# Where the rows of the first two groups are finished: part of a tuned spectral-filter and feed-forward kernel is moved into an earlier stage

## The chip, the cores and the metric

The kernel runs on one core of one Trainium2 chip. Its time is the device time of one execution in microseconds (us); the median of three runs of the kernel before is 159.57 us (159.57 to 159.85). The engines are TensorE (PE; its weight loads are listed as PEld), VectorE (DVE), ScalarE (ACT), GpSimd (POOL) and the sync engine (SP), whose queue issues the DMAs. Each engine carries out its own instructions in the order in which the program has them and waits on semaphores for the others.

## The reference

```
h   = x + irfft2( rfft2(layernorm(x)) * (w_r + i w_i) )       x: 1 x 2048 x 512, bf16
out = h + ( relu(layernorm(h) @ w1 + b1) ** 2 ) @ w2 + b2     w1: 512 x 1792, w2: 1792 x 512
```

The Fourier transforms are taken over rows and columns (2048 and 512) and are made of matrix products with tables of sines. h stands for the filtered rows; the second line is a feed-forward network, with a residual h and a bias b2 added to each output row.

## The kernel before, in words

The 2048 rows are 16 groups of 128 (row = 16 p + g), g = 0 to 15, with p on the partitions. The kernel has three runs, one behind the other.

The first run loads x, makes the tables, takes the statistics of the first layer norm and does the first transform steps.

The middle run (lines 508 to 772) goes over eight pairs of row frequencies, pr = 0 to 7. For each, TensorE makes p2 (lines 522 to 532) and p3 (573 to 600), ScalarE copies them out as U and AB, VectorE makes X (sums and differences), m (times the filter weights), Z and M (lines 607 to 653), TensorE makes p4 (655 to 685) and ScalarE copies it to T2 (687 to 700). Pair 7 comes last, and its p4 is made in two parts: "a" holds only what groups 0 and 1 need (copied by T2a-7), "b" the rest (T2b-7-0 and T2b-7-1). Groups 0 and 1 then get a short path of their own, so that the feed-forward part can start: pd (line 703) multiplies T2 by the inverse column table GI, EO (710) copies it out, yt (714 to 736) adds the filter result to the transposed x, sq, ss, sd and r2 (737 to 748) take the second layer norm's factor, and UT0 (750) is the normalised input of the feed-forward part, transposed. GI is scaled in place on GpSimd (line 495) after two DMA transposes have brought it.

The last run (lines 774 to 1001) works in five chunks of groups, (0,1), (2..4), (5..8), (9..12), (13..15). For chunk 0 the up products ph (line 949) read UT0; the first two of its fourteen are split by group, pf-0 and pf-1 for group 0, ph-0-0 and ph-0-1 for group 1. For each later group, p5 (814) and p6 (837) finish the filter, with od, q and R between them; hs is the row h. relu (962), squares (967), the down products po (978) and the output addition ot (988) follow; ot adds hb, which is h + b2. For chunk 0, hb is made from py (lines 875 to 892): three steps of products add x (an identity product), and two parts of the filter result in EO, and VectorE adds the bias b2b. That is done in the last run, at its beginning.

The order of the instructions on an engine is set by a planner, class Plan (line 34). Every step is a task with an estimated duration, what it reads and writes, and a priority; run() always takes the task that can start first. Where an order is written out by hand, in MID (line 760) for the middle run and DRAIN (line 995) for the beginning of the last, the planner follows it. SP and POOL have no written order: there priorities, estimated durations and the estimated time to landing ("lag") decide. The planner also puts in products of a zero tile fz (warm(), line 244; they compute nothing that is used) where it sees TensorE wait over 0.3 us.

PSUM has eight banks. In the middle run the pool psg holds two single banks (0 and 1), and psb three pairs of banks (2-3, 4-5, 6-7) for "mm" tiles. In the last run the pool ps2 has four single banks, 2 to 5, for p5, p6 and some of ph ("pp" and "ph" tiles), and pso has banks 6 and 7 for "po" tiles. Lines 774 and 778 to 779 change the pools; a tile of ps2 or pso may be written when the tile of psb that lay there has been read out (reuse_waits="tile"). Before, py is a "po" tile.

Of the kernel before, what the change touches and what calls it, by code (L numbers as in the profile page):

```python
# [9 lines left out]
ALU = mybir.AluOpType  # L10
ACT = mybir.ActivationFunctionType
# [4 lines left out]
P = 128  # L16
# [17 lines left out]
class Plan:  # L34
# [13 lines left out]
    def add(self, eng, w, fn, reads=(), writes=(), prio=0.0, alloc=None, at=0.0, shared=False, lag=0.0,  # L48
            uses=(), order=(), name=None):
        many = isinstance(eng, tuple)  # L50
        ways = dict(zip(eng, w)) if many else {eng: w}
        t = dict(many=many, eng=None, ways=ways, w=0.0, fn=fn, reads=list(reads), writes=list(writes), prio=prio, alloc=alloc, at=at,
                 shared=shared, lag=lag, end=None, order=list(order), n=len(self.tasks),
                 name=name or "-".join(map(str, writes[-1] if isinstance(writes[-1], tuple) else writes[-1:])))
        self.tasks.append(t)
        for k in t["writes"]:
            self.made.setdefault(k, []).append(t)
        for k in set(t["reads"]) | set(t["writes"]) | set(uses):
            self.use.setdefault(k, []).append(t)
# [85 lines left out]
def kernel(  # L145
# [52 lines left out]
    sq0 = persist.tile([P, 2, ND, P], BF16, name="sq0")  # L198
    rsb = persist.tile([P, 2, P], FP32, name="rsb")
    UT0 = persist.tile([P, 2, ND, P], BF16, name="UT0")  # L200
    EO = persist.tile([P, 2, 2, 256], BF16, name="EO")
    junk = persist.tile([P, D], BF16, name="junk")
    fz = persist.tile([P, 512], BF16, name="fz")
# [30 lines left out]
    psg = ps  # L234
# [7 lines left out]
    add = plan.add  # L242

    def warm(p):
        for _ in range(min(7 if psg is ps else 20, int(plan.gap * 0.6 / 0.0625)) if plan.gap > 0.3 else 0):
            mm(p[:, 0:P], lhsT=fz[:, 0:P], rhs=fz[:, 0:P], start=True, stop=True)  # L246

    def sg_tile(key):
# [44 lines left out]
    def pool(w, fn, prio, reads=(), writes=(), **k):  # L293
        add("POOL", w, fn, reads=reads, writes=writes, prio=prio, **k)
# [167 lines left out]
            order=[("EI", 3)], writes=[("EI", 3, pr)], prio=17, lag=6.0)  # L462
    for t in range(2):
        add("SP", 1.3, lambda t=t: sy.dma_start(GI[:, :, P * t:P * t + P], flat(GF[:, t]), transpose=True), reads=[("gf", t)],
            order=[("EI", 3)], writes=[("gi", t)], prio=40.5 + t / 10, lag=12.0)
    for k, (d, s) in ((0, (W1[:], B_w1.rearrange("(c p) f -> p c f", p=P))),
                      (1, (W2[:], B_w2.rearrange("(i p) d -> p i d", p=P))),
                      (3, (b2b[:], B_b2.unsqueeze(0).to_broadcast([P, D])))):
        add("SP", 0.7, lambda d=d, s=s: sy.dma_start(d, s), writes=[("FW", k)], prio=40 + k, lag=15.0,
            order=[("gi", 1)] * (k > 0) + [("EI", i) for i in range(4)] + [("Wr", 0), ("Wr", 1), ("Wn", 0), ("Wn", 1)])  # L470

    PE0 = 5
    BY_PE = tuple(range(PE0, 8))
# [7 lines left out]
    def mid_tasks():  # L481
        def b1t():
            p = sg_tile(("b1",))
            mm(p[:, 0:NF], lhsT=b1b[:], rhs=ident[0:NF, 0:NF], start=True, stop=True)
            for g in range(2):
                mm(p[0:2, P + P * g:2 * P + P * g], lhsT=nmh[:, g], rhs=ident[:], start=True, stop=True)
        act(0.19, lambda: sc.copy(nmt[:], T[("b1",)][0:2, P:3 * P].rearrange("p (g c) -> p g c", g=2)), 142.0, reads=[("b1",)],
            writes=["nmt"], name="nmt")
        add("PE", 0.2, b1t, reads=["b1b", "ident", "nmh"], order=[("p3", 3)], writes=[("b1",)], prio=141.0, alloc=("sg", ("b1",)))
        act(0.19, lambda: sc.copy(b1f[:], T[("b1",)][:, 0:NF]), 142.0, reads=[("b1",)], writes=["b1f"])  # L490
        act(1.4, lambda: sc.preload_act_table_set("natural_log_exp_and_others"), 0.0, reads=["eps"], writes=["sqrt"])

        pool(0.2, lambda: gp.memset(ones[:], 1.0), 400.0, writes=["ones"])
        for e in range(2):
            pool(0.5, lambda e=e: gp.tensor_scalar(GI[:, 1 + 2 * e], GI[:, 1 + 2 * e], hrow[:], 1.0, ALU.mult, ALU.mult), 410.0,  # L495
                 reads=["hv", ("gi", 0), ("gi", 1)], writes=["GI"], name=f"GI-{e}")
        pool(0.15, lambda: gp.tensor_copy(nmh[:, :, 0], nm1[:, 0:2]), 401.0, reads=["nm1"], writes=["nmh0"])
        pool(0.15, lambda: gp.tensor_tensor(nmh[:, :, 1], nm1[:, 0:2], nmh[:, :, 0], ALU.subtract), 402.0, reads=["nmh0"],
             writes=["nmh"])
# [218 lines left out]
        for d in range(ND):  # L718
            mm(T["yt", g][:, P * d:P * d + P], lhsT=xs[:, g, P * d:P * d + P], rhs=ident[:], start=False, stop=False)
    for g in range(2):  # L720
        add("PE", 0.22, lambda g=g: cen(g), reads=["ones", "nmt"], order=[("p3", 7)], writes=[("yt", g, 0)],
            uses=[("yt", g)], name=f"yt-{g}-0", prio=170.0, alloc=("sg", ("yt", g)))
        add("PE", 0.22, lambda g=g: res(g), reads=["ident"], order=[("yt", g, 0)], uses=[("yt", g)],
            writes=[("yt", g, 1)], name=f"yt-{g}-1", prio=170.0)

    for g in range(2):
# [23 lines left out]
        def ut0(g=g):  # L750
# [2 lines left out]
        dve(0.66, ut0, -30.0, reads=[("r2", 0, g)], uses=[("yt", g)],   # L753
            writes=[("UT", 0), "UT0b" if g else "UT0a"], name=f"UT0-{g}")

    def sq_of(src, g):
        sc.activation(junk[:], src, ACT.Square, bias=nm1[:, g:g + 1], accum_out=ss2[:, g:g + 1])  # L757

    T["UT", 0] = UT0
    MID = {  # L760
# [10 lines left out]
    }  # L771
    plan.run(MID)

# [26 lines left out]
    ONE = (1, 2, 3, 4)  # L800
    TURN = (2, *range(5, G))
    HBP = 0
    OWN = 1
    SPLIT = 2
    UPT = ("ph", "sg")

    for c, (a, b) in enumerate(CHUNKS):
# [64 lines left out]
                add(("DVE", "POOL")[HBP], (0.62, 1.3)[HBP], lambda g=g: (ve, gp)[HBP].tensor_tensor(hb[:, g, :], hs[:, g, :], b2b[:], ALU.add),  # L872
                    prio=late + 180 + g, reads=[("hs", g), ("FW", 3)], order=[("ph", c, 4)], writes=[("hb", g)])

        if c == 0:
            for g in range(2):
                def d6(g=g, k=0):
                    py = (bank(("py", g), "po", 2) if k == 0 else T["py", g])[:]
                    if k == 0:
                        mm(py, lhsT=ident[:], rhs=xs[:, g, :], start=True, stop=False)  # L880
                    elif k == 1:
                        mm(py, lhsT=KI[:, 0], rhs=EO[:, g, 0].unsqueeze(1).to_broadcast([P, 2, 256]), start=False, stop=False)
                    else:
                        mm(py[:, 0:256], lhsT=KI[:, 0], rhs=EO[:, g, 1], start=False, stop=False)
                        mm(py[:, 256:512], lhsT=KI[:, 1], rhs=EO[:, g, 1], start=False, stop=True)
                for k in range(3):
                    add("PE", 0.22, lambda g=g, k=k, d6=d6: d6(g, k), reads=[["ident"], [("EO", g), ("EI", 3)], [("EO", g)]][k],
                        order=[("yt", 1, 3)] + [("py", g, j) for j in range(k)], uses=[("py", g)],
                        writes=[("py", g, k)] + [("py", g)] * (k == 2), name=f"py-{g}-{k}", prio=-3000.0 + g,
                        alloc=None if k else ("po", ("py", g)))  # L890
                dve(0.69, lambda g=g: ve.tensor_tensor(hb[:, g, :], T["py", g][:], b2b[:], ALU.add), -10.0,
                    reads=[("py", g), ("FW", 3)], order=[("UT", 0)] * OWN, writes=[("hb", g)])
        else:
            z = late + 50
            for k, (p0, p1) in enumerate([(g, g + 1) for g in range(a, b)] if c in ONE else [(a, b)]):
                pool(0.15, lambda p0=p0, p1=p1: gp.tensor_scalar(rs2[:, p0:p1], ss2[:, p0:p1], 1.0 / D, EPS, ALU.mult, ALU.add),  # L896
# [76 lines left out]
        for i in range(n):  # L973
            g = a + i
            for h in range(2) if g == G - 1 else (None,):
# [9 lines left out]
                        writes=[("po", g, h), ("po", g, h, k)], uses=[("act", c)], prio=nxt(),  # L985
                        alloc=("po", ("po", g, h)) if k == 0 else None)

                def out_(g=g, h=h, cs=cs):
                    o = T["ot", g] if h else buf(ffn, ("ot", g), "ot", [P, D], BF16, 3)
                    ve.tensor_tensor(o[:, cs], T["po", g, h][:, cs], hb[:, g, cs], ALU.add)  # L990
                dve(0.66 if h is None else 0.42, out_, nxt(), reads=[("po", g, h), ("hb", g)], uses=[("ot", g)],
                    writes=[("ot", g, h)], alloc=None if h else ("ot", ("ot", g)))
                add("SP", 0.1, lambda g=g, cs=cs: sy.dma_start(ov[:, g, cs], T["ot", g][:, cs]), reads=[("ot", g, h)],
                    writes=[("out", g)], uses=[("ot", g)], prio=nxt())
    DRAIN = {
        "PE": "py-1-0 py-0-0 py-1-1 py-0-1 py-1-2 py-0-2 pf-0 pf-1 p5-2 ph-0-0 ph-0-1 p5-3 ph-0-5 "
             "ph-0-3 ph-0-2",
        "ACT": "od-2 rl-0-0 rl-0-1 od-3 rl-0-5",
        "DVE": "hb-1 hb-0 q-2-0 q-2-1",
    }  # L1000
    plan.run(DRAIN)
    pin(tc, nc)
# [29 lines left out]
```

## Time and profile before

| what | value |
|---|---|
| median of three runs | 159.57 us |
| the profiled execution: its time, its span | 158.99 us, 157.2 us |
| busy: TensorE, VectorE, ScalarE, GpSimd | 152.0, 116.4, 102.0, 37.7 us |
| granted TensorE clock | 1.0 |
| middle run's last VectorE step (M-7-1) ends | 43.5 us |
| first feed-forward product starts | 49.5 us |
| zero-tile products (L246) in all | 69, of which 10 behind the middle run's main part |

The span is the profiled part of the execution; 1.79 us lie around it. "L952" and the like are lines of the kernel. A busy figure is a sum over the span, so a stage has to be read for itself. The view of stretches gives the busy time of each engine between two moments; the chain of waits is followed back from the last instruction to what released each step; the timeline lists an engine's instructions with start, length, and the idle time ahead of them with what ended it.

### The profile page before, as it was taken

Reading aid. Unit: us, or ns where it says so; the run is one execution under the profiler, and the core shown is the slowest. Engines: PE = TensorE matmul, PEld = TensorE weight load, DVE = VectorE, ACT = ScalarE, POOL = GpSimd, SP = SyncE. Lnnn points to the kernel's source line nnn. Section 1 sums busy time; section 2 is a strip of 40 time slices with the busy share of each in tenths; the row PEclk is TensorE's granted clock in tenths of the full one; section 3 lists DMA queues with packets and bytes.
Section 4 is the critical chain, followed back from the end, with each engine's and each line's share of the span. In section 5 each row is a group of like instructions: output and inputs, shape, how many; then the busy total and the mean of one; then the engine's idle time right before and its main releaser. Section 6 shows DMA issues by size and latency. Waiting matters only on the chain.

```text
span 157.2 us, 2915 instructions
## 1 busy us (share of the span) xinstructions
PE 152.0 (97%) x1038; PEld 92.5 (59%) x1038; DVE 116.4 (74%) x310; ACT 102.0 (65%) x187; POOL 37.7 (24%) x84
## 2 busy tenths in 40 slices
PE   6998999999999999999999999999999999999992
PEld 4677876787788985556544544444544444555461
DVE  6999889999908987899832989981699963285221
ACT  8989689999767996599702889340688820288000
POOL 8898300005900024213400022530002340000000
PEclk9999999999999999999999999999999999999999
DMA  4957998799700001121121000324000412100011
GB/s 151 312 190 222 284 224 176 210 295 310 226 4 0 4 0 35 48 54 38 33 67 60 7 4 0 67 48 120 33 0 4 66 38 65 35 33 4 0 67 33
DMA packets 23449, 14.02 MB, mean 89 GB/s; under 512 B 12170, under 2 KB 22154, under 8 KB 23434
## 3 DMA queue, kind: packets, MB, share of 16 engines
q1 hardware_dynamic: 23434, 13.84, 33.5%
q8 instruction: 8, 0.13, 0.3%
q14 instruction: 7, 0.06, 0.1%
HBM read 8.92 MB, written 3.01 MB: 76 GB/s over the span
## 4 chain that ended last, share of the span: by engine, by line
PE 75%; DVE 14%; issue 3%; POOL 3%; DMA 2%; ACT 0%; DVEq 0%
PE po L981 31%; PE sg L952 20%; PE ph L952 11%; DVE Z L635 4%; DVE m L625 4%; DMA xs<-in_A_x_dram 2%; DVE X L611 2%; DVE st L395 2%; POOL KR L411 1%; PE pp L840 1%; DVE M L649 1%; DVE M L647 1%; POOL rs L402 1%; PE pp L847 1%; PE s_p L418 1%
## 5 line engine op out<-in xcount | busy, mean ns | idle before, releaser
L981 PE MATMUL po<-W,act 128*128 128x512 bf16 (+1 forms) x238 | 50.0, 367 | 0.0
L964 ACT ACTIVATE rl<-sg,b1f 128x512 bf16<-128x512 f32 (+2 forms) x46 | 27.4, 602 | 20.1 <-PE sg L952 19.1
L952 PEld LDWEIGHTS <-W 128*128 128x128 bf16 x288 | 26.9, 98 | 19.3
L952 PE MATMUL sg<-UT,W 128*128 128x512 bf16 (+3 forms) x188 | 37.6, 334 | 0.0
L981 PEld LDWEIGHTS <-act 128*128 128x128 bf16 x238 | 23.1, 98 | 24.3
L970 DVE TENSOR_TENSOR act<-rl 128x384 bf16<-128x384 bf16 (+2 forms) x70 | 25.2, 368 | 6.5 <-ACT rl L964 6.0
L990 DVE TENSOR_TENSOR ot<-po,hb 128x512 bf16<-128x512 f32 (+1 forms) x17 | 11.2, 660 | 22.0 <-PE po L981 21.9
L896 POOL TENSOR_SCALAR rs<-ss 128x1 f32<-128x1 f32 x14 | 5.8, 416 | 65.5 <-ACT junk L757 65.5
L952 PE MATMUL ph<-UT,W 128*128 128x384 bf16 (+3 forms) x100 | 20.5, 328 | 0.0
L964 ACT ACTIVATE rl<-ph,b1f 128x384 bf16<-128x384 f32 (+2 forms) x24 | 14.3, 596 | 8.2 <-PE ph L952 7.5
L757 ACT ACTIVATE junk<-hs,nm 128x512 bf16<-128x512 bf16 x14 | 10.0, 714 | 1.7 <-DVE hs L868 1.5
L868 DVE TENSOR_TENSOR hs<-pp,xs 128x512 bf16<-128x512 f32 x14 | 9.6, 689 | 1.8 <-PE pp L840 1.3
L495 POOL TENSOR_SCALAR GI<-GI,hrow 128x256 bf16<-128x256 bf16 x2 | 6.0, 2986 | 17.5 <-DMA GI<-GF 17.5
L506 PE MATMUL m_p<-U,EF 128*128 128x512 bf16 (+1 forms) x46 | 9.5, 337 | 0.0
L863 DVE TENSOR_TENSOR R<-q 128x127 bf16<-128x127 f32 x40 | 9.3, 285 | 0.0
L872 DVE TENSOR_TENSOR hb<-hs,b2b 128x512 f32<-128x512 bf16 x14 | 9.2, 684 | 0.0
L395 DVE BATCH_NORM_STATS2 st<-xs 128x6 f32<-128x512 bf16 x14 | 9.0, 672 | 0.1
L898 POOL TENSOR_TENSOR rs<-rs,mhalf 128x1 f32<-128x1 f32 x14 | 8.3, 596 | 1.2
L689 ACT CAST T<-m_p 128x1024 bf16<-128x1024 f32 (+1 forms) x8 | 7.5, 955 | 0.8 <-PE m_p L673 0.7
L908 ACT ACTIVATE u<-hs,nr,rs 128x512 bf16<-128x512 bf16 x5 | 4.1, 811 | 5.9 <-POOL nr L900 5.9
L246 PEld LDWEIGHTS <-fz 128*128 128x128 bf16 x69 | 5.5, 108 | 3.8 <-issue 1.6
L830 DVE TENSOR_TENSOR q<-pp,od 128x256 f32<-128x256 f32 x20 | 7.7, 417 | 0.0
(154 smaller groups left out, 230.4 us busy)
## 6 DMA issues: line engine op xcount, KB each, us to landing
W<-in_B_w_dram SPq DMA_DIRECT2D x2, 1792.0 KB, 8.5
out_dram<-ot SPq DMA_DIRECT2D x15, 128.0 KB, 1.8
xs<-in_A_x_dram SPq DMA_DIRECT2D x4, 256.0 KB, 3.6
xs<-in_A_x_dram SPq DMA_DIRECT2D x2, 512.0 KB, 6.1
W<-wx SPq DMA_DIRECT2D x2, 448.0 KB, 5.1
W<-in_A_w_r_dram SPq DMA_DIRECT2D x1, 512.0 KB, 8.6
W<-in_A_w_i_dram SPq DMA_DIRECT2D x1, 512.0 KB, 6.1
wx<-in_A_w_r_dram SPq DMA_DIRECT2D x1, 448.0 KB
```

The source lines that it names most:

```text
L395: ve.bn_stats(st[:], xs[:, g, :])
L506: mm(o.rearrange("p (j i e) -> p j i e", e=2, i=RUN), lhsT=w, rhs=U[:, q, s].rearrange("p (j e i) -> p j i e", e=2, i=RUN), **k)
L757: sc.activation(junk[:], src, ACT.Square, bias=nm1[:, g:g + 1], accum_out=ss2[:, g:g + 1])
L863: ve.tensor_tensor(o, x, y, (ALU.add, ALU.subtract, ALU.subtract, ALU.add)[k])
L868: dve(0.66, lambda g=g: ve.tensor_tensor(hs[:, g, :], T["p6", g][:], xs[:, g, :], ALU.add), z, reads=[("p6", g)], writes=[("hs", g)])
L872: add(("DVE", "POOL")[HBP], (0.62, 1.3)[HBP], lambda g=g: (ve, gp)[HBP].tensor_tensor(hb[:, g, :], hs[:, g, :], b2b[:], ALU.add), prio=lat ...
L898: pool(0.57, lambda p0=p0, p1=p1: gp.tensor_tensor(rs2[:, p0:p1], rs2[:, p0:p1], mhalf[:, 0:p1 - p0], ALU.pow), z, reads=[("sd", c, k)], w ...
L952: mm(p[:, P * i0:P * i1], lhsT=W1[:, d, bass.ts(f, P)], rhs=T["UT", c][:, i0:i1, d, :], start=(d == 0), stop=(d == ND - 1))
L964: sc.activation(r[:, 0:P * n], T["ph", c, f][:, 0:P * n], ACT.Relu, bias=b1f[:, f:f + 1], scale=1.0)
L970: ve.tensor_tensor(t[:, f, 0:P * n], r[:, 0:P * n], r[:, 0:P * n], ALU.mult)
L981: mm(p[:, cs], lhsT=T["act", c][:, f, bass.ts(i, P)], rhs=W2[:, f, cs], start=(f == 0), stop=(f == NF - 1))
L990: ve.tensor_tensor(o[:, cs], T["po", g, h][:, cs], hb[:, g, cs], ALU.add)
```

## The change

The rows hb of groups 0 and 1 are made in the middle run. A new tile hb0 (128 x 2 x 512, FP32) first gets x + b2, from two GpSimd additions (tasks xb). py is now two steps of products (the identity products with x are gone) in an "mm" tile of psb, and VectorE adds py and hb0 into hb0 (hb-0, hb-1), behind UT0 in the written order. The output addition reads hb0 for chunk 0.

For that the bias DMA comes ahead of W2's on SP's queue and behind the two GI transposes. Two planner figures change: the lag of the GI transposes (12.0 to 7.5) and the duration of the GI scaling on GpSimd (0.5 to 2.9). warm() puts in products only in the first run (psg is ps there alone). yt-0-0 and yt-1-0 get another place in the planner's rules. MID and DRAIN are new: T2a-7 goes from ScalarE to VectorE, T2b-7-1 on ScalarE comes ahead of sq-0, and p5-3, p5-4 and p5-2 come ahead of pf-1, pf-0 and ph-0-0 on TensorE. Behind these written orders the planner is free.

```diff
+    hb0 = persist.tile([P, 2, D], FP32, name="hb0")
     def warm(p):
-        for _ in range(min(7 if psg is ps else 20, int(plan.gap * 0.6 / 0.0625)) if plan.gap > 0.3 else 0):
+        for _ in range(min(7, int(plan.gap * 0.6 / 0.0625)) if plan.gap > 0.3 and psg is ps else 0):
...
-            order=[("EI", 3)], writes=[("gi", t)], prio=40.5 + t / 10, lag=12.0)
+            order=[("EI", 3)], writes=[("gi", t)], prio=40.5 + t / 10, lag=7.5)
...
-        add("SP", 0.7, lambda d=d, s=s: sy.dma_start(d, s), writes=[("FW", k)], prio=40 + k, lag=15.0,
-            order=[("gi", 1)] * (k > 0) + [("EI", i) for i in range(4)] + [("Wr", 0), ("Wr", 1), ("Wn", 0), ("Wn", 1)])
+        add("SP", 0.7, lambda d=d, s=s: sy.dma_start(d, s), writes=[("FW", k)], prio=40.7 if k == 3 else 40 + k, lag=10.0 if k == 3 else 15.0,
+            order=[("gi", 1)] * (k > 0) + [("FW", 3)] * (k == 1) + [("EI", i) for i in range(4)] + [("Wr", 0), ("Wr", 1), ("Wn", 0), ("Wn", 1)])
...
-            pool(0.5, lambda e=e: gp.tensor_scalar(GI[:, 1 + 2 * e], GI[:, 1 + 2 * e], hrow[:], 1.0, ALU.mult, ALU.mult), 410.0,
+            pool(2.9, lambda e=e: gp.tensor_scalar(GI[:, 1 + 2 * e], GI[:, 1 + 2 * e], hrow[:], 1.0, ALU.mult, ALU.mult), 410.0,
...
-        add("PE", 0.22, lambda g=g: cen(g), reads=["ones", "nmt"], order=[("p3", 7)], writes=[("yt", g, 0)],
+        add("PE", 0.22, lambda g=g: cen(g), reads=["ones", "nmt"], order=[("p4", 7, "a", 0)] if g == 0 else [("p4", 7, "b", 0)], writes=[("yt", g, 0)],
...
+    for g in range(2):
+        pool(1.3, lambda g=g: gp.tensor_tensor(hb0[:, g, :], xs[:, g, :], b2b[:], ALU.add), 420.0 + g,
+             reads=[("x", g), ("FW", 3)], writes=[("xb", g)])
+
+        def d6(g=g, k=0):
+            py = (T["py", g] if k else mm_tile(("py", g)))[:, 0:512]
+            if k == 0:
+                mm(py, lhsT=KI[:, 0], rhs=EO[:, g, 0].unsqueeze(1).to_broadcast([P, 2, 256]), start=True, stop=False)
+            else:
+                mm(py[:, 0:256], lhsT=KI[:, 0], rhs=EO[:, g, 1], start=False, stop=False)
+                mm(py[:, 256:512], lhsT=KI[:, 1], rhs=EO[:, g, 1], start=False, stop=True)
+        for k in range(2):
+            add("PE", 0.22, lambda g=g, k=k, d6=d6: d6(g, k), reads=[("EO", g), ("EI", 3)], order=[("py", g, 0)] * k,
+                writes=[("py", g, k), ("py", g)], name=f"py-{g}-{k}", prio=-3000.0 + g, alloc=None if k else ("mm", ("py", g)))
+        dve(0.69, lambda g=g: ve.tensor_tensor(hb0[:, g, :], T["py", g][:, 0:512], hb0[:, g, :], ALU.add), -10.0,
+            reads=[("py", g), ("xb", g)], writes=[("hb", g)])
...
     MID = {
-        "PE": "p3-1 p2-2-0 p2-2-1 p2-4-0 p2-4-1 p2-3-0 p3-2 p2-3-1 p3-4 p2-6-0 p2-6-1 p3-3 p4-0-0 b1 "
-             "p4-0-1 p3-6 p2-5-0 p2-5-1 p2-7-0 p2-7-1 p4-2-0 p4-2-1 p4-1-0 p4-1-1 p3-5 p3-7 p4-3-0 "
-             "p4-3-1 p4-4-0 p4-4-1 p4-6-0 yt-0-0 p4-6-1 p4-5-0 yt-0-1 p4-5-1 p4-7-0a p4-7-1a p4-7-0b "
-             "pd-0 pd-1 yt-1-0 yt-1-1 yt-0-2 yt-0-3 yt-1-2 yt-1-3 p4-7-1b ss-0 ss-1",
-        "ACT": "AB-1 U-2 U-4 AB-2 U-3 AB-4 U-6 b1f AB-3 nmt T2-0 AB-6 U-5 U-7 T2-2 sqrt AB-5 T2-1 AB-7 "
-              "T2-3 T2-4 T2-6 T2-5 T2a-7 EO-0 EO-1 sq-0 sq-1 sd-0-0 r2-0-0 sd-0-1 r2-0-1 T2b-7-1",
-        "DVE": "m-0-0 m-0-1 Z-0-0 Z-0-1 X-1-0 X-1-1 m-1 Z-1-0 Z-1-1 M-1-0 X-2-0 X-2-1 M-1-1 m-2 X-4-0 "
-              "Z-2-0 X-4-1 Z-2-1 m-4 M-2-0 Z-4-0 X-3-0 M-2-1 X-3-1 Z-4-1 m-3 M-4-0 Z-3-0 Z-3-1 m-6 "
-              "M-4-1 M-3-0 Z-6-0 M-3-1 m-5 Z-6-1 Z-5-0 Z-5-1 m-7 M-5-0 M-5-1 Z-7-0 Z-7-1 M-7-0 M-7-1 "
-              "T2b-7-0 UT0-0 UT0-1",
+        "PE": "p3-1 p2-2-0 p2-2-1 p2-3-0 p2-3-1 p2-5-0 p3-2 p2-5-1 p3-3 p2-4-0 b1 p2-4-1 p3-5 p4-0-0 "
+             "p4-0-1 p2-7-0 p2-7-1 p2-6-0 p3-4 p4-2-0 p2-6-1 p4-2-1 p4-1-0 p4-1-1 p3-6 p4-3-0 p3-7 "
+             "p4-3-1 p4-5-0 p4-5-1 p4-6-0 p4-4-0 p4-4-1 p4-6-1 p4-7-0a yt-0-0 p4-7-1a p4-7-0b yt-0-1 "
+             "pd-0 pd-1 yt-1-0 p4-7-1b yt-0-2 yt-0-3 yt-1-1 yt-1-2 yt-1-3 ss-0 py-1-0 ss-1 py-0-0 "
+             "py-1-1 py-0-1",
+        "ACT": "AB-1 U-2 U-3 AB-2 U-5 nmt AB-3 b1f U-4 AB-5 T2-0 U-7 AB-4 U-6 T2-2 T2-1 AB-6 sqrt AB-7 "
+              "T2-5 T2-3 T2-4 T2-6 EO-0 EO-1 T2b-7-1 sq-0 sq-1 sd-0-0 r2-0-0 sd-0-1 r2-0-1",
+        "DVE": "m-0-0 m-0-1 Z-0-0 Z-0-1 X-1-0 X-1-1 m-1 Z-1-0 Z-1-1 M-1-0 X-2-0 X-2-1 M-1-1 m-2 X-3-0 "
+              "Z-2-0 Z-2-1 X-3-1 M-2-0 M-2-1 m-3 m-5 Z-3-0 Z-5-0 Z-3-1 X-4-0 M-3-0 Z-5-1 M-3-1 X-4-1 "
+              "M-5-0 m-4 M-5-1 Z-4-0 Z-4-1 m-6 M-4-0 Z-6-0 m-7 M-4-1 Z-6-1 Z-7-0 Z-7-1 M-7-0 M-7-1 "
+              "T2a-7 T2b-7-0 UT0-0 UT0-1 hb-0 hb-1",
     }
...
-        if c == 0:
-            for g in range(2):
-                def d6(g=g, k=0):
-                    py = (bank(("py", g), "po", 2) if k == 0 else T["py", g])[:]
-                    if k == 0:
-                        mm(py, lhsT=ident[:], rhs=xs[:, g, :], start=True, stop=False)
...
-                dve(0.69, lambda g=g: ve.tensor_tensor(hb[:, g, :], T["py", g][:], b2b[:], ALU.add), -10.0,
-                    reads=[("py", g), ("FW", 3)], order=[("UT", 0)] * OWN, writes=[("hb", g)])
-        else:
+        if c:
...
-                    ve.tensor_tensor(o[:, cs], T["po", g, h][:, cs], hb[:, g, cs], ALU.add)
+                    ve.tensor_tensor(o[:, cs], T["po", g, h][:, cs], (hb if c else hb0)[:, g, cs], ALU.add)
...
     DRAIN = {
-        "PE": "py-1-0 py-0-0 py-1-1 py-0-1 py-1-2 py-0-2 pf-0 pf-1 p5-2 ph-0-0 ph-0-1 p5-3 ph-0-5 "
-             "ph-0-3 ph-0-2",
-        "ACT": "od-2 rl-0-0 rl-0-1 od-3 rl-0-5",
-        "DVE": "hb-1 hb-0 q-2-0 q-2-1",
+        "PE": "p5-3 p5-4 p5-2 pf-1 pf-0 ph-0-0",
+        "ACT": "od-3 od-2",
     }
```

More of the change, by code (lines that the diff above doesn't have):

```diff
@@ L802 @@
     HBP = 0
-    OWN = 1
     SPLIT = 2
@@ L873 @@
                     prio=late + 180 + g, reads=[("hs", g), ("FW", 3)], order=[("ph", c, 4)], writes=[("hb", g)])
-        if c == 0:
-            for g in range(2):
-                def d6(g=g, k=0):
-                    py = (bank(("py", g), "po", 2) if k == 0 else T["py", g])[:]
-                    if k == 0:
-                        mm(py, lhsT=ident[:], rhs=xs[:, g, :], start=True, stop=False)
-                    elif k == 1:
-                        mm(py, lhsT=KI[:, 0], rhs=EO[:, g, 0].unsqueeze(1).to_broadcast([P, 2, 256]), start=False, stop=False)
-                    else:
[L884 to L891, printed above, removed]
-                    reads=[("py", g), ("FW", 3)], order=[("UT", 0)] * OWN, writes=[("hb", g)])
-        else:
+        if c:
             z = late + 50
@@ L986, with out_ @@
                         alloc=("po", ("po", g, h)) if k == 0 else None)
-                def out_(g=g, h=h, cs=cs):
+                def out_(c=c, g=g, h=h, cs=cs):
                     o = T["ot", g] if h else buf(ffn, ("ot", g), "ot", [P, D], BF16, 3)
-                    ve.tensor_tensor(o[:, cs], T["po", g, h][:, cs], hb[:, g, cs], ALU.add)
+                    ve.tensor_tensor(o[:, cs], T["po", g, h][:, cs], (hb if c else hb0)[:, g, cs], ALU.add)
                 dve(0.66 if h is None else 0.42, out_, nxt(), reads=[("po", g, h), ("hb", g)], uses=[("ot", g)],
```

## The prediction, made before the changed kernel ran

> **What bounds the kernel now.** I read the page's busy line, then the stretches around the change, then the chain of waits from 43 to 51 us, then the timelines of the other engines there. The busy line:
>
> ```profile
> PE 152.0 (97%) x1038; PEld 92.5 (59%) x1038; DVE 116.4 (74%) x310; ACT 102.0 (65%) x187; POOL 37.7 (24%) x84
> ```
>
> The stretches (length, then busy time of each engine, granted clock):
>
> ```profile
> 22.00:43.60 21.60, 21.32 (x180) 15.97 (x179) 21.25 (x44) 20.10 (x23) 5.96 (x2) 1.00 0.92 233
> 43.60:49.60 6.00, 6.00 (x62) 4.64 (x63) 1.78 (x3) 4.47 (x11) 0.00 (x0) 1.00 0.01 3
> 51.04:58.20 7.16, 7.16 (x88) 6.63 (x86) 6.82 (x23) 6.63 (x18) 0.96 (x3) 1.00 0.01 2
> 58.20:157.20 99.00, 96.00 (x528) 49.00 (x525) 65.58 (x176) 51.57 (x105) 15.90 (x39) 1.00 0.15 38
> ```
>
> Up to 43.6 us VectorE is full (21.25 of 21.60), and TensorE and ScalarE nearly so. From 43.6 on TensorE never rests (6.00 of 6.00, 7.16 of 7.16, and 96 of 99 with the tail). So a microsecond of TensorE work taken out behind 43.6 counts in full, if the next work is ready; and a microsecond in which TensorE must stand still there is lost for good. The chain of waits (start, length, work), in the piece that the change rebuilds:
>
> ```profile
> 43.59 0.27 PE s_p L675 x4
> 43.85 0.39 PE m_p L675 x4
> 44.24 0.39 PE m_pd L246 x7
> 44.63 0.87 PE m_pd L707 x8
> ...
> 47.66 0.17 PE m_ss L246 x3
> 47.83 0.32 PE m_ss L743 x4
> 48.15 0.56 PE po L880 x2
> 48.71 0.43 PE po L882 x2
> ...
> 49.58 0.28 PE ph L952 x4
> ```
>
> L246 are the zero-tile products, L880 the x products of the two output rows, L952 the first feed-forward product. And the other engines' timeline in the same place:
>
> ```profile
> 43.99 0.27 ACT L692 CAST T<-s_p 128x128 bf16<-128x128 f32 x1
> 46.63 1.09 ACT L737 ACTIVATE sq<-s_yt 128x512 bf16<-128x512 f32 x2 [0.45 <-PE s_yt L730]
> 48.44 1.29 DVE L751 TENSOR_TENSOR UT<-s_yt,rsb 128x512 bf16<-128x512 f32 x2 [0.37 <-ACT rsb L747]
> 49.65 1.28 DVE L891 TENSOR_TENSOR hb<-po,b2b 128x512 f32<-128x512 f32 x2
> ```
>
> The reader is to see that VectorE reads the two py tiles (L891) only at 49.65 to 50.93, behind UT0. Before, nobody waits for that.
>
> **What is taken out.** Ten zero-tile products (0.39 + 0.17) and the two x products (512 columns each, as L882: 0.43 for two): 0.56 + 0.43 = 0.99 us of TensorE. If TensorE stayed full, that is -0.99.
>
> **The middle run's new orders.** The same VectorE instructions in another order can win at most the idle of 22 to 43.6 us, 0.35; I walked the written orders with these durations (m 1.14, other VectorE steps 0.34, ScalarE copies 0.91, p2 half 0.44, p3 0.87 or 1.74, p4 half 0.44). m-7 again starts at some 39.8, behind AB-7 at 39.3. One doubtful place: M-3-0 (34.2) needs M-1's buffer, which p4-1-1 frees at some 34.4. I take 0, bounds -0.35 and +0.5. The cover is thin: any later stall on VectorE here goes straight into T2a.
>
> **The chain from M-7-1 to UT0.** T2a-7 moves from ScalarE to VectorE, which is free then; ScalarE had T2-5 in hand to 43.99, while the product ended at 43.85. With 0.29 (VectorE's nearest row, 256 columns to bf16 in 0.285; ScalarE 0.27) it ends at 44.2, so pd-0 starts at 44.27, not 44.47 behind the zero products. EO-0 and EO-1 (1.07) then end at 45.99. T2b-7-1 (0.51) moves into ScalarE's 0.45 wait ahead of sq-0; its product is done by 45.9 (pd 0.87, yt-1-0 0.22, p4-7-1b 0.39). So sq-0 starts at 46.45 instead of 46.63. All behind it keeps its distances: UT0-1 ends at 49.55, hb-0 at 50.15, hb-1 at 50.75, each 0.18 earlier.
>
> **x plus bias on GpSimd.** Two new additions 128x512. They queue behind GI on POOL. The near row:
>
> ```profile
> L495 POOL TENSOR_SCALAR GI<-GI,hrow x2: 883/2986/5090, 37.0 to 42.0; 128x256 bf16<-128x256 bf16 x2
> ```
>
> The first took 5.09 us beside a full VectorE, the second 0.88 as VectorE ran out. The Trainium skill, "GPSIMD Engine Reference", section "Performance versus the Vector engine", puts a two-input addition at half VectorE's speed and 4497 ns for 2048 elements, an estimate of 1.12 us for 512; its "Key points" say that GpSimd contends with VectorE instructions that read two SBUF inputs. That speaks against the change. By the rows: 2 x 0.88 = 1.77 each at best, 10.2 each at worst. They run from 42.9, when VectorE has just 0.6 us of two-SBUF-input work left and then stands for 3.92, so I take the page's 1.1 to the row's 1.8: done by 45.2 to 46.5, against the need at 49.55. Cover 3 us, cost 0; at the worst row hb-1 would end at 64. The bias itself must be there: its DMA now goes to SP's queue ahead of W2 instead of behind it. The DMA records show W1, then the two gi transposes (landed at 36.96), then W2's and the bias' 1 KB packets to some 42; so the bias lands near 38 and W2, 128 packets later, near 42, used at 58. Cost 0, and GI's landing is not changed.
>
> **The wait that is added.** This decides. py-0 and py-1 are no longer "po" tiles: they are "mm" tiles of psb, the three bank pairs that ps2 and pso take over. In the program of before, an mm tile always takes the pair of the tile that ScalarE read out first: this gives the listed banks of all 25 mm tiles of the middle run. The same rule over the new orders gives p4-7b banks 6-7, pd-0 and ss-0 2-3, pd-1 and py-1 4-5, ss-1 6-7, and py-0 2-3. ps2 covers banks 2 to 5. Its first tiles, p5-3, p5-4 and p5-2, are written ahead of pf-1 and pf-0, and a fresh tag of three takes its first, last and middle bank (pp before: 3, 5, 4): 2, 4, 3. So p5-3 waits for hb-0's read of bank 2 and p5-4 for hb-1's read of bank 4. Before, p5-2 ran on a bank released by T2b.
>
> TensorE is through py-0-1 by some 48.7 (pd-0 44.27 + pd 0.87, yt-1-0 0.22, p4-7-1b 0.39, yt 0.43 + 0.22 + 0.43 = 46.83; ss-0 waits for sq-0, 47.1; then ss 0.22, py-1-0 0.22, ss-1 behind sq-1, 47.6 to 47.9; py 0.65). It stands to 50.2 (1.5 us), p5-3 0.22, stands to 50.8 (0.4), then p5-4, p5-2, pf-1, pf-0, ph-0-0, ph-0-1, each 0.22: done at 52.12. Queued behind the wait is the whole feed-forward. Before, two p5, two pf, two ph are done at 50.82, the third p5 would make it 51.04. **Sum:** 52.12 - 51.04 = +1.08. The 0.99 taken out are in it: they come off time that is now waited for anyway. From here TensorE is full to the end and shifts as a whole. The profiled execution's 158.99 (span 157.2, 1.79 around it) becomes 160.07; the median of the runs is 0.58 above it, so 159.57 + 1.08 = **160.7**.
>
> If ps2 instead kept the tag "ph" in bank 2, pf-0 would wait for hb-0 and p5-2 (bank 4) for hb-1: 51.9, +0.9. If only p5-3 were held, +0.5. With the middle's -0.3 to +0.5 this gives the likeliest case its own range, 160.0 to 161.5.
>
> A second rule: "TensorE: Matmul & The Clock Gate" (Part 1 and "HAM oscillation") says that the clock is halved after gaps over some 3.4 us. The row: granted clock 1.00 in every stretch, with gaps of at most 0.2 us in the middle run. My stand of 1.5 us stays below it; should the clock fall, some 3.4 us of products would take double, +3.4. I take 0.
>
> **Rivals.** (a) *No bank wait*: placement sets py beside the p5 tiles. Then py ends at 48.7, three p5 fill the time to UT0-1 (49.55), pf and ph end at 50.2: -0.84, 158.7. For it speaks that p5 ahead of pf makes sense only so; against it the 25 banks. It decides when neither py lies in 2 to 5, which the release order excludes unless two copies change places. (b) *The middle run gets late*: a buffer or PSUM wait in the new orders, or GI slow twice, beyond 0.7: M-7-1 or GI at 44.5 or more, 161.5 to 163. For it: 0.35 us of slack on VectorE; against it: the walk finds only M-3-0. (c) *GpSimd late*: above 3.3 us per addition (42.9 to 49.55 for two) hb is held; at 5 us each hb-1 ends at 53.6, +4. Against it: VectorE stands for 3.92 there.
>
> **How the numbers follow.** Likeliest 0.80, (a) 0.12, (b) 0.06, (c) 0.02. 0.2% (0.32 us) is about what a measurement of this kernel can tell from no change. Faster: (a) and a sliver, 0.13; same: 0.04, the weak wait with a lucky middle; slower 0.83. Range 159.8 to 161.8: nearly all of the likeliest case and the near end of (b); (a) is what it leaves out.
>
> **What would show it.** In the changed profile: TensorE idle 1 to 2 us ahead of the first L817 to L820 products, at 50.2, released by VectorE's hb line; the first L952 near 51.3, not 49.5; two POOL additions hb0<-xs,b2b of 1.1 to 1.8 us from 42.9; UT0 starting near 48.25; no m_pd or m_ss in L246. Wrong if L952 starts before 50, or if UT0 moves by over 0.5.

## The result, and the profile after

The changed kernel takes 161.59 us (161.43 to 162.71, four runs) against 159.57 us before: a ratio of 1.014, 95% interval 1.0092 to 1.0188. It is slower, as forecast, and inside the range of 159.8 to 161.8, but by 2.0 us (1.5 to 3.0 by the interval) where 1.1 were forecast: the bank wait came as forecast, but the chain ahead of it, from M-7-1 to sq, was put 1.0 us too short. The profiled execution is the slowest of the four (162.71, about 1.1 us above the others): its TensorE clock was granted at 0.50 from 52.0 to 55.0 us and was back at 1.0 from 55.3 on. Times up to 51 us are not touched by that.

The page's busy line of the changed kernel:

```profile
PE 152.7 (95%) x1026; PEld 92.6 (58%) x1026; DVE 116.9 (73%) x312; ACT 101.2 (63%) x185; POOL 41.5 (26%) x86
```

TensorE's busy time rose by 0.7 us, although 0.99 us of work was taken out, because products take longer at half the clock. The stretches of the changed kernel (length, busy time of each engine, granted clock, DMA):

```profile
43.60:49.60 6.00, 5.32 (x52) 3.97 (x52) 1.30 (x3) 4.18 (x10) 2.37 (x3) 1.00 0.01 3
49.60:53.00 3.40, 1.74 (x19) 1.51 (x18) 2.10 (x4) 0.86 (x3) 0.00 (x0) 0.84 0.00 0
53.00:60.00 7.00, 7.00 (x71) 6.30 (x70) 4.89 (x17) 5.40 (x14) 0.00 (x0) 0.83 0.01 2
```

TensorE rested nowhere behind 43.6 us before. Now it rests 0.68 us in the first of these stretches and 1.66 us in the second; from 53 on it is full again. (0.84 and 0.83 are means over the stretches; the 0.50 lies within them.) TensorE's timeline of the changed kernel shows for whom (start, length, work, and in brackets the idle time ahead with what ended it):

```profile
43.39 0.39 PE L716 MATMUL s_yt<-nmt,ones 2*128 2x512 bf16 x1
43.71 0.27 PE L676 MATMUL s_p<-EI,M 128*128 128x32 bf16 x4
...
44.43 1.04 PE L708 MATMUL m_pd<-GI,T 128*128 128x256 bf16 x8
...
48.05 0.38 PE L744 MATMUL m_ss<-sq,ones 128*128 128x128 bf16 x4 [0.68 <-ACT sq L738]
...
49.43 0.27 PE L767 MATMUL m_py<-EO,KI 128*128 128x256 bf16 x1
51.16 0.22 PE L835 MATMUL pp<-GI,T 128*128 128x127 bf16 x1 [1.45 <-DVE hb L771]
...
51.76 0.22 PE L835 MATMUL pp<-GI,T 128*128 128x127 bf16 x1 [0.21 <-DVE hb L771]
...
52.45 0.63 PE L952 MATMUL sg<-UT,W 128*128 128x128 bf16 x4
```

L835 is the first product of p5-3 and of p5-4, and each waits for VectorE's hb line: the bank wait. The first feed-forward product comes at 52.45 instead of 49.48; part of that is order, since three p5 now run ahead of it. The first two lines are yt-0-0 and p4-7-1a, which come up again below. The other engines in the same place, from the timelines of VectorE, ScalarE and GpSimd:

```profile
43.06 0.41 DVE L650 TENSOR_TENSOR M<-Z 128x512 bf16<-128x512 bf16 x1
44.01 0.29 DVE L693 CAST T<-s_p 128x128 bf16<-128x128 f32 x1 [0.54 <-PE s_p L676]
46.31 0.62 DVE L690 CAST T<-m_p 128x448 bf16<-128x448 f32 x1 [2.01 <-PE m_p L676]
46.97 0.53 ACT L690 CAST T<-m_p 128x448 bf16<-128x448 f32 x1 [0.83 <-DVE T L690]
47.40 1.09 ACT L738 ACTIVATE sq<-s_yt 128x512 bf16<-128x512 f32 x2
49.22 1.29 DVE L752 TENSOR_TENSOR UT<-s_yt,rsb 128x512 bf16<-128x512 f32 x2 [2.28 <-ACT rsb L748]
50.42 1.28 DVE L771 TENSOR_TENSOR hb<-m_py,hb 128x512 f32<-128x512 f32 x2
43.70 2.26 POOL L758 TENSOR_TENSOR hb<-xs,b2b 128x512 f32<-128x512 bf16 x2
```

The first line is M-7-1, the second T2a-7. The fourth, ScalarE's copy at 46.97, is what the prediction missed. ScalarE's half of the T2b copy, which was to fill a wait, waits 0.83 us itself, at the end for VectorE's half of the same PSUM tile (46.31 to 46.93), and only then does sq start: at 47.40, where 46.45 was forecast.

### The profile page after: what moved, and what is told of

The parts are those of the page before. It is cut to its first block, busy times and chain, and to the rows that moved or that the text cites. A ratio compares the mean times of both kernels' runs of the same rounds, so it can differ in the third digit from the quotient of the medians.

```text
span 160.9 us, 2895 instructions
## 1 busy us (share of the span) xinstructions
PE 152.7 (95%) x1026; PEld 92.6 (58%) x1026; DVE 116.9 (73%) x312; ACT 101.2 (63%) x185; POOL 41.5 (26%) x86
## 4 chain that ended last, share of the span: by engine, by line
PE 73%; DVE 16%; POOL 3%; issue 3%; ACT 2%; DMA 2%; DVEq 0%
PE po L981 30%; PE sg L952 20%; PE ph L952 11%; DVE m L626 5%; DVE Z L636 3%; DMA xs<-in_A_x_dram 2%; DVE st L396 2%; DVE X L612 2%; DVE M L648 2%; POOL KR L412 1%; PE pp L858 1%; POOL rs L403 1%; PE pp L865 1%; PE s_p L419 1%; DVE M L650 1%
## 5 line engine op out<-in xcount | busy, mean ns | idle before, releaser
L952 PEld LDWEIGHTS <-W 128*128 128x128 bf16 x288 | 28.0, 102 | 19.5
L952 PE MATMUL sg<-UT,W 128*128 128x512 bf16 (+3 forms) x188 | 38.3, 341 | 0.0
L952 PE MATMUL ph<-UT,W 128*128 128x384 bf16 (+3 forms) x100 | 21.0, 338 | 0.0
L496 POOL TENSOR_SCALAR GI<-GI,hrow 128x256 bf16<-128x256 bf16 x2 | 7.1, 3560 | 17.1 <-DMA GI<-GF 17.1
L605 ACT CAST AB<-m_p 128x1024 bf16<-128x1024 f32 x7 | 7.1, 1010 | 0.9 <-PE m_p L507 0.8
L528 PE MATMUL m_p<-GF,Bt 128*128 128x256 bf16 x56 | 7.3, 273 | 0.0
```

The lines of the kernel that those rows point to most:

```text
L952: mm(p[:, P * i0:P * i1], lhsT=W1[:, d, bass.ts(f, P)], rhs=T["UT", c][:, i0:i1, d, :], start=(d == 0), stop=(d == ND - 1))
```

## The experiments

Two theories were put side by side: that p5 lies on py's banks and TensorE stands for hb (bank theory), and that the new orders or the missing zero products make the loss and the stand only shows it. Since the first part of the kernel ends up to 0.7 us earlier or later from execution to execution, moments are compared below by their distance from the end of M-7-1 (43.47 us in the changed kernel, 43.53 before). The line of before:

```profile
43.12 0.41 DVE L649 TENSOR_TENSOR M<-Z 128x512 bf16<-128x512 bf16 x1
```

**py moved off p5's banks.**

```diff
-            py = (T["py", g] if k else mm_tile(("py", g)))[:, 0:512]
+            py = (mm_tile(("py",)) if g and not k else T[("py",)])[:, 512 * g:512 * g + 512]
...
-             ... ss-0 py-1-0 ss-1 py-0-0 py-1-1 py-0-1
+             ... ss-0 ss-1 py-1-0 py-0-0 py-1-1 py-0-1
```

> The changed kernel with py-0 and py-1 in the two halves of one PSUM tile, taken behind ss-1, so that it lies in banks 6 and 7 and no p5 tile lies over it; all else as in the changed kernel. Bank theory (TensorE stands for hb because p5 lies on py's banks): the stands of 1.45 and 0.21 us ahead of p5 go, p5-3 starts near 49.6 us, the first feed-forward products are through near 51.2 instead of 53.1, and the time falls by some 1.9, to 159.7. Rival theory (the new middle orders, or the missing zero products, make the loss, and the stand is only where it shows): TensorE then stands for something else in the same place, and the time stays within 0.4 of 161.6.

Measured: 159.63 us, ratio to the kernel before 1.0009 (0.9998 to 1.0021), so the stand was worth 2.0 us. VectorE's M-7-1 and TensorE's timeline in this run:

```profile
43.65 0.41 DVE L650 TENSOR_TENSOR M<-Z 128x512 bf16<-128x512 bf16 x1
...
50.10 0.27 PE L767 MATMUL m_py<-EO,KI 128*128 128x256 bf16 x1
50.21 0.22 PE L835 MATMUL pp<-GI,T 128*128 128x127 bf16 x1
...
50.89 0.39 PE L952 MATMUL sg<-UT,W 128*128 128x128 bf16 x4
```

p5-3 follows py without a rest (6.15 us behind M-7-1, where the changed kernel has 7.69), and VectorE's hb, at 51.01 in this run, holds nobody. UT0 starts 5.74 behind M-7-1 (49.80) where the changed kernel has 5.75 (49.22), so the chain itself did not move. The bank theory stands; the rival expected 161.2 or more.

The rests listed in the changed kernel come to 1.66 us, yet 2.0 was lost. A rest is counted from the end of the last product (0.27 for the one at 49.43), while in a full queue the next product starts 0.11 behind the start of such a product. Without the waits p5-3 would have started at 49.54, not 51.16, and p5-4 at 51.38, not 51.76: 1.62 and 0.38, together 2.0.

**Both halves of T2b on VectorE.**

```diff
-  ACT: ... EO-0 EO-1 T2b-7-1 sq-0 sq-1 ...
-  DVE: ... T2a-7 T2b-7-0 UT0-0 UT0-1 hb-0 hb-1
+  ACT: ... EO-0 EO-1 sq-0 sq-1 ...
+  DVE: ... T2a-7 T2b-7-0 T2b-7-1 UT0-0 UT0-1 hb-0 hb-1
```

> The changed kernel with T2b-7-1 on VectorE, behind T2b-7-0, instead of on ScalarE ahead of sq-0. Theory that the copy holds the chain (ScalarE's copy waited 0.83 us for VectorE's half of the same PSUM tile): sq-0 starts near 46.75 instead of 47.40, UT0 and hb move forward by 0.65, and p5-3 with them, so the time falls by 0.65, to 160.9. Rival (the chain is not what hb waits for, GpSimd's addition or py is): UT0 moves and hb does not, and the time stays at 161.6.

Measured: 161.03 us, 1.0107 (1.0085 to 1.0129), 0.56 below the changed kernel. VectorE's M-7-1, and ScalarE's and TensorE's timelines:

```profile
43.48 0.41 DVE L650 TENSOR_TENSOR M<-Z 128x512 bf16<-128x512 bf16 x1
47.17 1.26 ACT L738 ACTIVATE sq<-s_yt 128x512 bf16<-128x512 f32 x2 [0.61 <-PE s_yt L731]
51.00 0.22 PE L835 MATMUL pp<-GI,T 128*128 128x127 bf16 x1 [1.45 <-DVE hb L771]
```

M-7-1 ended at 43.89 here, so sq starts 3.28 behind it instead of 3.93, and p5-3 7.11 instead of 7.69. The stand ahead of p5-3 is the same 1.45: TensorE and hb moved forward together, as the theory says. Of the 0.65 that sq-0 gained, 0.58 reached p5-3: the two sq now take 1.26 us instead of 1.09, the second waiting for its yt. The intervals of the changed kernel and of this run overlap, so 0.56 alone is not clear of noise; the run with both edits gives the same 0.6 a second time, clear of noise.

**Both (e3_both).** The two edits together.

> Both edits of the two runs before. If the bank wait and the late copy are two separate parts of the loss: UT0-1 ends near 49.9, the first feed-forward products are through near 50.6, and the time is about 159.1, 2.5 below the changed kernel and 0.5 below the kernel before, which is what the 0.99 us of removed products can give less what TensorE waits for sq. If the middle orders lose besides: 159.6 or more.

Measured: 159.02 us, 0.9976 (0.9967 to 0.9985). The two parts add up: 2.0 and 0.6 from 161.6. Against the first of the two edits alone (159.63) it is 0.61 faster, with intervals that do not touch. In TensorE's timeline the one rest over 0.2 us that is left is a wait for sq (0.28):

```profile
48.65 0.38 PE L744 MATMUL m_ss<-sq,ones 128*128 128x128 bf16 x4 [0.28 <-ACT sq L738]
...
49.74 0.22 PE L835 MATMUL pp<-GI,T 128*128 128x127 bf16 x1
...
50.42 0.39 PE L952 MATMUL sg<-UT,W 128*128 128x128 bf16 x4
```

**hb-0 ahead of UT0, py in the wait for sq, both ss sums in one tile.**

```diff
-  PE: ... p4-7-0a yt-0-0 p4-7-1a p4-7-0b yt-0-1 pd-0 pd-1 yt-1-0 p4-7-1b ... yt-1-3 ss-0 py-1-0 ss-1 py-0-0 py-1-1 py-0-1
-  DVE: ... T2b-7-0 UT0-0 UT0-1 hb-0 hb-1
+  PE: ... p4-7-0a p4-7-1a yt-0-0 p4-7-0b yt-0-1 pd-0 pd-1 p4-7-1b yt-1-0 ... yt-1-3 py-0-0 ss-0 py-0-1 py-1-0 ss-1 py-1-1
+  DVE: ... T2b-7-0 T2b-7-1 hb-0 UT0-0 UT0-1 hb-1
```

> A version meant to keep what the change takes out: T2b-7-1 on VectorE, p4-7-1a ahead of yt-0-0, the py products in TensorE's wait for sq, hb-0 on VectorE ahead of UT0, both ss sums in one PSUM tile so that py-1 lies in banks 6 and 7. Bank and chain theory: pd starts near 44.2, UT0-1 ends near 49.7, the first feed-forward products are through near 50.3, no stand above 0.3 us for hb: 158.8. Rival (VectorE's hb-0 ahead of UT0 delays the chain by its 0.6): 159.4.

Measured: 159.13 us, 0.998 (0.9969 to 0.999), no better than the run before it, and neither the 158.8 of the one theory nor the 159.4 of the other. TensorE and ScalarE:

```profile
44.71 1.04 PE L708 MATMUL m_pd<-GI,T 128*128 128x256 bf16 x8
...
48.59 0.38 PE L744 MATMUL m_ss<-sq,ones 128*128 128x128 bf16 x4
49.01 0.37 ACT L746 ACTIVATE rsb<-m_ss,eps 128x128 f32<-128x128 f32 x1
```

ss-1 starts at 48.59, though sq-1 had ended at 48.28: it follows the end of ScalarE's first rsb step on the shared tile (48.54). The shared tile has become a wait of up to 0.3. A second loss stands ahead of it: pd starts 1.20 behind M-7-1 (which ended at 43.51), where the run with both edits has 0.95, since p4-7-0b and yt-0-1 are still in front of it, and sq-0 is 0.24 later too. Which of the two losses, or VectorE's hb-0 ahead of UT0, used up the gain was not tried one by one.

**pd as early as possible.** py in one tile, T2b on VectorE, and on TensorE p4-7-1a ahead of yt-0-0, with p4-7-0b, p4-7-1b and yt-0-1 behind pd.

```diff
+  PE: ... p4-7-0a p4-7-1a yt-0-0 pd-0 pd-1 yt-0-1 p4-7-0b p4-7-1b yt-0-2 yt-0-3 yt-1-0 yt-1-1 yt-1-2 yt-1-3
+      py-1-0 ss-0 py-1-1 py-0-0 py-0-1 ss-1
```

> The last version again (py in one tile in banks 6 and 7, both T2b copies on VectorE), with TensorE's order behind M-7-1 changed so that pd starts as soon as T2a is copied: p4-7-1a ahead of yt-0-0, p4-7-0b and yt-0-1 behind pd, the py products in TensorE's wait for sq. If the chain T2a, pd, EO, yt, sq still sets part of the time: pd starts 0.7 us behind M-7-1's end instead of 0.95, TensorE's rests behind 43.6 us fall below 0.3 in all, and the time is 158.6, 0.4 below e3_both. If TensorE's own work is all that counts there: within 0.15 of e3_both, 159.0.

Measured: 159.24 us, 0.998 (0.9971 to 0.9989): the first theory missed, nothing was won over 159.02. T2a ended 0.65 behind M-7-1 (0.83 in the changed kernel) and pd did start 0.76 behind M-7-1 (0.95 in the run with both edits), but two other waits took it back:

```profile
47.98 0.60 ACT L738 ACTIVATE sq<-s_yt 128x512 bf16<-128x512 f32 x1 [0.49 <-PE s_yt L731]
49.71 0.22 PE L835 MATMUL pp<-GI,T 128*128 128x127 bf16 x1 [0.23 <-ACT rsb L746]
```

The second sq now waits for yt-1-3, and p5-4 for ss-1's bank.

**What the removed products are worth in the kernel before.** Only the zero-tile products behind the first run are taken out:

```diff
-        for _ in range(min(7 if psg is ps else 20, int(plan.gap * 0.6 / 0.0625)) if plan.gap > 0.3 else 0):
+        for _ in range(min(7, int(plan.gap * 0.6 / 0.0625)) if plan.gap > 0.3 and psg is ps else 0):
```

> The kernel before, with the zero-tile products behind the first run taken out and nothing else (10 products, 0.56 us of TensorE). Chain theory (they stand partly in waits for T2a, sq and UT0): 0.35 to 0.45 faster than the kernel before, 159.05. If TensorE's work alone counts: 0.56 faster, 158.9. If they hide wholly in waits: no change.

Measured: 159.44 us, 0.999 (0.9981 to 1.0). The gain is 0.1 to 0.2 of the 0.56, and the interval reaches down to none; of the three theories, that the products hide wholly in waits comes closest.

**x plus bias on GpSimd in the kernel before, without the x products.** py stays in banks 6 and 7; the bias DMA goes ahead of W2 and the two planner figures change, both as in the change.

```diff
+        pool(1.3, lambda g=g: gp.tensor_tensor(hb0[:, g, :], xs[:, g, :], b2b[:], ALU.add), 420.0 + g,
+             reads=[("x", g), ("FW", 3)], writes=[("xb", g)])
...
-                        mm(py, lhsT=ident[:], rhs=xs[:, g, :], start=True, stop=False)
```

> The kernel before, with x plus bias on GpSimd and without the two x products (0.43 us of TensorE), py still in banks 6 and 7 of the last run, old orders, bias DMA ahead of W2. UT0-0 is ready 0.35 us ahead of pf-0 in the kernel before, so up to that much counts: 0.3 to 0.4 faster, 159.1. Rival (GpSimd's additions or the moved DMA cost something): same or slower than before.

Measured: 160.49 us, 1.0052 (1.0034 to 1.0069), slower by 0.8 (by the ratio) to 0.95 (by the medians). VectorE, GpSimd and TensorE:

```profile
43.75 1.37 DVE L650 TENSOR_TENSOR M<-Z 128x512 bf16<-128x512 bf16 x1
43.52 2.61 POOL L758 TENSOR_TENSOR hb<-xs,b2b 128x512 f32<-128x512 bf16 x2
45.17 0.27 PE L676 MATMUL s_p<-EI,M 128*128 128x32 bf16 x4 [1.03 <-DVE M L650]
```

M-7-1 (two SBUF inputs) takes 1.37 us where it takes 0.41 otherwise: GpSimd's addition, which also reads two SBUF inputs, had begun 0.23 us ahead of it. The whole chain behind it is 0.96 late. GpSimd was slowed as well: its two additions took 2.61 us instead of 2.26.

**Both of these together (e8_xbnowarm).**

> The kernel before with the edits of both runs: no zero-tile products behind the first run, x plus bias on GpSimd, no x products; old orders and banks. 0.99 us of TensorE is taken out. Chain theory: the chain to UT0 moves by only 0.15 to 0.2, so no more than 0.35 + 0.2 counts, 0.5 faster than before, 158.9, not the sum of the two. If TensorE's work alone counts: 1.0 faster, 158.4.

Measured: 160.36 us, 1.0045 (1.0029 to 1.0062), with the same 1.37 us. So the worth of the 0.99 us of products cannot be read from these two. The next run takes away the collision alone:

```diff
+    pool(0.2, lambda: gp.tensor_copy(scr[:], T["M", 7][:, 1, 1, 255:256]), 419.0, reads=[("M", 7)], writes=["scr"])
...
-             reads=[("x", g), ("FW", 3)], writes=[("xb", g)])
+             reads=[("x", g), ("FW", 3), "scr"], writes=[("xb", g)])
```

> e8_xbnowarm with one tiny GpSimd copy from M-7's tile ahead of the two x plus bias additions, so that they start behind VectorE's last step M-7-1 instead of beside it; all else the same. In e8 M-7-1 took 1.37 us instead of 0.41 because GpSimd's addition began 0.25 us ahead of it. Collision theory: M-7-1 takes 0.41 again, all behind it moves forward by 0.96, and the time is 159.4, just below the kernel before. Rival (the moved bias DMA or the removed products cost the time): it stays at 160.3.

Measured: 159.31 us, 0.9995 (0.9975 to 1.0015). The stretch behind the middle run, then VectorE, GpSimd, TensorE:

```profile
43.60:49.60 6.00, 5.42 (x52) 3.86 (x51) 1.86 (x4) 4.59 (x11) 2.41 (x3) 1.00 0.02 5
43.24 0.41 DVE L651 TENSOR_TENSOR M<-Z 128x512 bf16<-128x512 bf16 x1
43.86 2.26 POOL L760 TENSOR_TENSOR hb<-xs,b2b 128x512 f32<-128x512 bf16 x2
49.45 0.38 PE L957 MATMUL ph<-UT,W 128*128 128x128 bf16 x4 [0.33 <-ACT T L691]
```

The collision is shown: M-7-1 is back at 0.41, and 0.8 (by the ratios) to 1.05 us (by the medians) comes back. The first and the last line show why 0.99 us of removed products win next to nothing in the old orders. TensorE now rests 0.58 us in the stretch (5.42 of 6.00), for steps of the chain that came only 0.15 earlier, and 0.33 of it is pf-0's wait for the T2b copy on ScalarE, which reads out the bank that pf-0 takes. A bank wait of this kind was already there in the kernel before, hidden behind the products: T2b ended at 49.42 and pf-0 started at 49.48.

```profile
48.91 0.51 ACT L689 CAST T<-m_p 128x448 bf16<-128x448 f32 x1
49.48 0.38 PE L952 MATMUL ph<-UT,W 128*128 128x128 bf16 x4
```

**py between the two ss sums.** The version with both edits, with py-1's products in TensorE's wait for sq; the PSUM tiles are taken in such an order that py still has banks 6 and 7.

```diff
-             p = mm_tile(("ss", g))
+             if not g:
+                 mm_tile(("ss", 0)), mm_tile(("ss", 1)), mm_tile(("py",))
+                 mm(T["ss", 1][:, P:2 * P], lhsT=fz[:, 0:P], rhs=fz[:, 0:P], start=True, stop=True)
+             p = T["ss", g]
...
-  PE: ... ss-0 ss-1 py-1-0 py-0-0 py-1-1 py-0-1
+  PE: ... ss-0 py-1-0 py-1-1 ss-1 py-0-0 py-0-1
```

> e3_both with one py group's products moved between the two ss sums on TensorE, into its wait for sq (the PSUM tiles of ss and py are taken together, and one zero-tile product is added, so that py stays in banks 6 and 7). If TensorE's rests of some 0.5 us in that place are what is left: 0.3 to 0.4 below e3_both, 158.7. If UT0 is by then the later one: the same as e3_both, 159.0.

Measured: 158.85 us, 0.996 (0.9947 to 0.9973), the fastest of these versions; the 0.17 to the run with both edits is not clear of noise. The stretch and TensorE's timeline:

```profile
43.60:49.60 6.00, 5.96 (x63) 4.57 (x64) 2.29 (x5) 4.32 (x10) 2.74 (x3) 1.00 0.01 3
```

```profile
49.28 0.22 PE L838 MATMUL pp<-GI,T 128*128 128x127 bf16 x1
...
49.96 0.39 PE L955 MATMUL sg<-UT,W 128*128 128x128 bf16 x4
```

TensorE is full again behind 43.6 us (5.96 of 6.00), with p5 done ahead of the feed-forward products. The change pays once nothing waits for hb.

## Why the prediction was right or wrong, point by point

**The bank wait: right, with its place and its size.** p5-3 and p5-4 stand for hb-0 and hb-1, for 1.45 and 0.21 us (forecast 1.5 and 0.4; counted from start to start, as above, 1.62 and 0.38). Their length held although hb came 1.0 us later, because py, ahead of them on TensorE, waits for sq too and came later by as much. The changed program has py-0 in bank 2, py-1 in bank 4, p5-3, p5-4 and p5-2 in 2, 4 and 3, as worked out from the release order. With py elsewhere the time falls by 2.0.

**From M-7-1 to sq: this step failed.** The prediction moved T2b-7-1 into ScalarE's wait ahead of sq-0 at no cost, and moved yt-0-0 and yt-0-1 at no cost. It put sq-0 at 2.92 us behind M-7-1's end (46.45 - 43.53); it came at 3.93 (47.40 - 43.47), 1.01 later. Behind sq the distances held: hb-0 ended 3.70 us behind sq-0's start, as forecast. Its own sign of being wrong, UT0 moving by over 0.5, came true: UT0 started at 49.22, where 48.25 was forecast. Of the 1.01:
- 0.66 is "T2b-7-1 moves into ScalarE's wait ahead of sq-0". Both copies read one PSUM tile, on two engines; ScalarE's began only when VectorE's had ended (46.93), not when the product had (46.3). With both halves on VectorE sq-0 comes 0.65 earlier, and 0.56 to 0.61 of the time comes back. The wait is one that the program sets: in the program as built, ScalarE's copy has a semaphore wait for VectorE's, in the kernel before too, because the two read one tile (its two halves lie in two banks, 6 and 7). Before the change ScalarE's half came last on ScalarE, 0.84 behind the end of VectorE's, and the wait cost nothing.
- 0.22 is pd, 0.96 behind M-7-1 instead of 0.74. Most of it (0.16) is already in T2a, which ended at 44.30, 0.83 behind M-7-1 instead of 0.67: yt-0-0 (0.32) stood in front of p4-7-1a on TensorE, which so started only at 43.71. The rest is p4-7-0b and yt-0-1 in front of pd. Before, yt-0-0 and yt-0-1 ran ahead of M-7-0, under VectorE's cover. The run with pd as early as possible, with these three moved, has pd at 0.76.
- 0.10 is yt-1-0, costed at 0.22 where the row of before had 0.32.

1.08 + 0.98 is 2.06; 2.02 was measured, with an interval of 1.5 to 3.0, so that the fit is this close is partly luck. Only the first term was taken out by itself and timed. The other two are read from the timelines; they were not tried alone in the changed kernel, and a small further loss is not excluded.

**The 0.99 us taken out: right that they win nothing there.** The runs on the kernel before show more: zero products alone are worth 0.1, and all 0.99 us with the collision taken away 0.1 (interval -0.25 to +0.4), because TensorE then waits for the chain and for T2b's bank. With the waits removed and TensorE full, the best version is 0.6 below before.

**The middle run's new orders: right at 0.** M-7-1 ended 21.49 us behind the start of m-0-1 (21.98 to 43.47), before 21.69. M-3-0 did not stall.

**GpSimd's additions: right in price, right in cover, wrong in what was looked for.** 1.13 us each, where the estimate from the Trainium skill's "GPSIMD Engine Reference" (Performance versus the Vector engine) was 1.12 and the row's 1.77, done at 45.96, 4.5 us ahead of hb-0 (50.42). But the contention that the prediction read as GpSimd being slowed acts the other way too: GpSimd slows VectorE by 0.96. In the changed kernel the additions escape it by 0.23 us, since GI ended at 43.70, behind M-7-1. The prediction let them start at 42.9, ahead of M-7-1; by the 0.96 of these runs (an estimate) that would have cost about 1 us, which it put at 0. That they started later was luck.

**The clock: wrong in one execution of four.** The prediction took no fall, since its stand of 1.5 us lies below 3.4. In the profiled execution the clock did fall, to 0.50 for some 3.4 us (51.9 to 55.3). Its price for that case, +3.4, was also twice too high: half the clock over 3.4 us takes 1.7 us of TensorE time, and the execution was 1.1 us above the other three.

**The rivals.** (a) with no bank wait fell; its number, 158.7, is close to what the best version gives (158.85). (b) fell as it was put: M-7-1 ended on time (43.47), and what got late was the chain behind it. (c) fell: the additions took 1.13 us each, not over 3.3.

## What to carry to other kernels

When a PSUM tile moves to another pool, look up which later tile gets its banks and which engine reads it out last: work that is written early as a filler waits for that reader, and all behind it on the in-order queue. A copy divided between two engines may run one behind the other if both read one tile; keep them on one engine (0.6 us here), or give each half its own tile (not tried here). A step taken off the critical engine pays only up to the next wait, so cost the moved fillers by the cover that they lose.

## What the runs showed of the hardware that was not expected

GpSimd's 128x512 addition with two SBUF inputs, begun 0.23 us ahead of a VectorE instruction with two SBUF inputs, made that instruction 1.37 us long instead of 0.41, twice, and 0.41 again when it was made to start behind it. GpSimd's additions themselves took 2.61 us instead of 2.26 there. The other way, GI's first scaling took 5.1 us beside a full VectorE before and 6.2 us after, 0.88 us for the second.

The granted TensorE clock was 0.50 from 52.0 to 55.0 us in one of the changed kernel's four executions, behind rests of 0.68, 1.45 and 0.21 us within 4.4 us; over the whole span the mean was 0.989 there and 0.999 or 1.0 in the other three, and 0.998 with the same 1.45 us rest in the profiled run with both halves of T2b on VectorE. So rests shorter than the 3.4 us that the prediction went by were followed by a slower clock, at some 1.1 us here; what decides between the executions stays open.
